# Turning q and k in separate tiles, with casts and PSUM copies split by head halves over VectorE and ScalarE

## The chip, the cores and the metric

One core of a Trainium2 chip. The metric is the device time of one execution in microseconds (us). In profile lines PE is TensorE, PEld its weight loads, DVE is VectorE, ACT is ScalarE, POOL is GpSimd. "PEclk" is the share of TensorE's full clock that was granted. SBUF and PSUM are the two on-chip memories that the program uses: PE's results are written to PSUM and copied from there to SBUF. A *tile* is a buffer that the program takes from a *pool*; the waits between instructions that use one tile are put in when the program is built (in the kernel before, ACT's copy out of a PSUM tile waits four times for DVE's copy out of it, 15.4 us in the first 85 us). A *hole* is a stretch in which PE is idle. *Bank* is the word for a size: a one-bank (single-bank) PSUM tile has 2 KB per partition (`[P, 4, 2, P]` in bf16), a two-bank tile 4 KB (`[P, 2, 4, 2, P]`).

## The reference

Sliding-window causal attention (batch 8, 8 heads, 576 tokens, head size 64, window 64), whose output of 4608 tokens x 512 goes through an up-projection to 2048, a quick GELU and a down-projection. The kernel takes and gives float32.

```python
scores = (1 / np.sqrt(D)) * np.matmul(q, k.transpose(0, 1, 3, 2))
mask = (rel >= 0) & (rel < 64)                 # rel = query position - key position
attn = softmax(np.where(mask, scores, -1e9))
x = np.matmul(attn, v).transpose(0, 2, 1, 3).reshape(B * S, H * D)
h = x @ w_in
out = (h * (1 / (1 + np.exp(-1.702 * h)))) @ w_out
```

## The kernel before

Attention works on blocks of 128 tokens (numbered m), the projections on chunks of four blocks. The program's scores take q and k with the head dimension on the partitions. For the first two batches this is done on chip. A *pair* is a load of q and k of 256 tokens (64 for a batch's third pair). It is cast to bf16 in SBUF, turned by 8 transposes of q and 8 of k on PE into PSUM, and copied from PSUM to `qkt` in SBUF. Later batches are turned by DMA and are not touched by the change.

```python
qkt = [keep.tile([P, 8, PAD + S], bf16, name=f"qkt{i}") for i in range(2)]   # q and k interleaved
DA = (nc.vector, nc.scalar)

def turn_mm(b, i, w, tiles):            # w = 0: q, 1: k
    n = pairs(i)
    for r in range(2):
        for hp in range(4):             # hp: a pair of heads
            nc.tensor.transpose(
                out=tiles[w][:, hp, r, 0:n],
                in_=rows[b % 2][w][0:n, 2 * i + r, P * hp : P * hp + P],
                identity=ident[0:n, 0:n])

def turn_out(b, i, w, tiles):           # DVE copies all of q, ACT all of k
    n = pairs(i)
    copy_on(DA[w],
        out=qkt[b % 2][:, w::2, PAD + 256 * i : PAD + 256 * i + 2 * n].rearrange(
            "p g (n r) -> p g n r", r=2),
        in_=tiles[w][:, :, :, 0:n].rearrange("p g r n -> p g n r"))

def turn_tiles(pool, tag):
    if pool is psT:                     # one tile for both: q in one half, k in the other
        t = pool.tile([P, 2, 4, 2, P], bf16, name="turn", tag=tag)
        return [t[:, 0], t[:, 1]]
    return [pool.tile([P, 4, 2, P], bf16, name="turn", tag=tag) for _ in range(2)]
# ... (scores, exp, mask, pv, norm, the turn of x, up and down) ...
```

Each engine's instructions stand in the order in which the program writes them: with the cast of the second pair written ahead of the first mask, DVE starts them at 11.01 and 11.92 us in the kernel before. Two stretches matter: the *opening* (the first four blocks, up to about 26 us), and the *seam* between the first chunk's down-projection and the second chunk's up-projection (about 47 to 63 us). `warm(n)` issues n small matmuls of no use to the result, to keep PE busy.

```python
# the seam; i counts the 16 steps of the first chunk's down-projection
        if i == 11: cast_pairs(1, 0, DA); ...
        if i == 12: turn_pairs(1, 0, turn_tiles(psT, "T"))
        if i == 14: scores(4); exp(4); down_out(0, 0); down_out(0, 1, on_dve=True); cast_v(1, 1)
        down(0, tsub, j, ...)
    mask(4); scores(5); pv(4); norm(4); exp(5)
    cast_pairs(1, 1, (nc.gpsimd, nc.scalar))
    down_out(0, 2); down_out(0, 3, on_dve=True)
    mask(5)
    x_mm(4, psT, "T"); x_out(4)
    turn_pairs(1, 1, turn_tiles(psT, "T"))
```

The softmax here doesn't subtract the row's maximum and nothing guards it: scores larger than these inputs give would overflow.

## Time and profile before

| | before |
|---|---|
| time, median of the first 3 runs (range) | 319.25 us (319.15 to 319.6) |
| profiled run: time, span, mean granted clock | 318.37 us, 316.6 us, 0.992 |
| PE's idle time in the span | 21.6 us |

The page's totals, the waits, the chain and part of the timeline are in the prediction below. What it doesn't show is the table of windows: for the opening, for the first chunk's up- and down-projection, and for the seam with what follows it, how long each engine was busy (in brackets the number of instructions).

```profile
core 0: us, PE busy (x) PEld busy (x) DVE busy (x) ACT busy (x) POOL busy (x), PEclk, DMA share, GB/s
0.00:26.00 26.00, 18.20 (x316) 15.89 (x317) 15.18 (x32) 13.30 (x16) 13.76 (x29) 0.93 1.06 207
26.00:44.00 18.00, 17.40 (x92) 9.07 (x93) 9.06 (x14) 7.76 (x13) 3.41 (x5) 1.00 1.00 218
44.00:90.00 46.00, 41.06 (x683) 32.59 (x687) 28.71 (x46) 27.86 (x43) 32.89 (x46) 1.00 0.97 177
```

No engine but PE is near full in any of these windows (PE has 17.40 of 18.00 us in the second; the fullest of the others is POOL in the third, 32.89 of 46.00), so what can be won is waiting: 7.8 us of PE's idle time lie before 26 us, 4.9 us between 44 and 90 us. Two rows of the timeline serve as landmarks (start, duration, instruction): the exponential of the first block, and the first up-projection matmuls after the scores of block 6, which end the seam.

```profile
10.10 1.02 ACT L272 ACTIVATE E<-S 128x1024 bf16<-128x1024 f32 x1 [0.50 <-PE S L262]
...
61.76 1.98 PE L349 MATMUL hps<-xT_pe,w_in_sb 128*128 128x128 bf16 x32
```

### The profile page before, as it was taken

How to read it: one execution, taken by the hardware profiler on the slowest of the kernel's cores; microseconds unless marked ns; L12 is line 12 of the kernel's file. 1: busy time of each engine (PE TensorE's matmuls, PEld its weight loads, DVE VectorE, ACT ScalarE, POOL GpSimd, SP SyncE). 2: the span in 40 equal slices, each digit the busy share in tenths (PEclk: the TensorE clock that was granted, in tenths of full speed). 3: DMA queues.
4: the chain of work that ended last, by engine and by line, in shares of the span. 5: the costliest groups of instructions: out<-in, count | busy, mean ns of one | idle time of the engine just before them, and what ended most of it. 6: DMA issues, size and time to landing. Idle time of an engine off the chain costs nothing.

```text
span 316.6 us, 7896 instructions
## 1 busy us (share of the span) xinstructions
PE 295.0 (93%) x3269; PEld 196.1 (62%) x3306; DVE 164.0 (52%) x276; ACT 157.4 (50%) x241; POOL 136.7 (43%) x195
## 2 busy tenths in 40 slices
PE   5688998599999999999999999999999999999994
PEld 5575444598777777777777777765554455444441
DVE  6556713687655555565565665555555554434300
ACT  2556514677655556545555555554444444344311
POOL 1870248474995796885669897120000000000000
PEclk9989999999999999999999999999999999999998
DMA  8999898898999999999999999955332111000121
GB/s 192 218 211 214 184 278 155 217 180 169 143 124 142 166 157 131 160 170 163 171 165 172 163 163 160 159 127 124 86 84 68 50 52 50 33 35 33 58 78 66
DMA packets 150996, 43.32 MB, mean 137 GB/s; under 512 B 135088, under 2 KB 145328, under 8 KB 150960
## 3 DMA queue, kind: packets, MB, share of 16 engines
q0 software_dynamic: 72480, 13.05, 64.1%
q1 hardware_dynamic: 74448, 22.43, 42.1%
q10 hardware_dynamic: 4032, 7.34, 6.6%
q8 instruction: 26, 0.43, 0.6%
q14 instruction: 10, 0.08, 0.1%
HBM read 36.70 MB, written 9.44 MB: 146 GB/s over the span
## 4 chain that ended last, share of the span: by engine, by line
PE 86%; ACT 4%; DVE 3%; issue 2%; DMA 2%; SPq 1%; ACTq 0%
PE ops L379 38%; PE hps L349 38%; PE Tacc L291 4%; PE S L262 4%; DMA stage_qk<-in_q_dram 2%; DVE gT L366 1%; PE turn L146 1%; ACT th L360 1%; ACT xT_pe L330 1%; DVE qkt L104 1%; PE pxt L325 1%; SPq L85 1%; ACT qkt L104 1%; DVE PT L277 1%; DVE xs L304 0%
## 5 line engine op out<-in xcount | busy, mean ns | idle before, releaser
L366 DVE SCALAR_TENSOR_TENSOR gT<-th,hps 128x512 bf16<-128x512 bf16 x144 | 98.9, 688 | 109.8 <-ACT th L360 109.6
L379 PE MATMUL ops<-w_out_sb,gT 128*128 128x512 bf16 x539 | 136.4, 379 | 5.4 <-issue 4.3
L360 ACT ACTIVATE th<-hps 128x512 bf16<-128x512 f32 x144 | 86.0, 597 | 110.7 <-PE hps L349 104.1
L349 PEld LDWEIGHTS <-w_in_sb 128*128 128x128 bf16 x1328 | 106.1, 113 | 40.9 <-issue 1.4
L379 PEld LDWEIGHTS <-gT 128*128 128x128 bf16 x576 | 53.0, 98 | 52.1 <-issue 0.8
L349 PE MATMUL hps<-xT_dma,w_in_sb 128*128 128x256 bf16 (+1 forms) x448 | 82.5, 318 | 0.0
L349 PE MATMUL hps<-xT_pe,w_in_sb 128*128 128x128 bf16 (+1 forms) x880 | 64.7, 228 | 1.1 <-ACT xT_pe L330 0.9
L272 ACT ACTIVATE E<-S 128x1024 bf16<-128x1024 f32 x36 | 36.7, 1019 | 2.7 <-PE S L262 2.7
L393 ACT ACTIVATE o_sb<-ops 128x512 f32<-128x512 f32 x34 | 20.4, 600 | 18.3 <-PE ops L379 18.0
L186 POOL COPY v_off<-v_nat 64x528 bf16<-64x528 bf16 x25 | 16.1, 646 | 27.9 <-DMA v_nat<-in_v_dram 27.3
L304 DVE TENSOR_TENSOR xs<-Tacc,rc 128x512 bf16<-128x512 f32 x36 | 24.9, 691 | 1.2
L182 POOL DMA_DIRECT2D v_nat<-in_v_dram x25 | 21.5, 859 | 2.3 <-issue 1.4
L277 DVE TENSOR_TENSOR PT<-E,mask_None 128x1024 bf16<-128x1024 bf16 x28 | 20.7, 738 | 2.4 <-ACT E L272 2.4
L181 POOL DMA_DIRECT2D rows_k<-in_k_dram x25 | 21.3, 853 | 0.0
L181 POOL DMA_DIRECT2D rows_q<-in_q_dram x25 | 21.3, 850 | 0.0
L262 PE MATMUL S<-qkt 64*128 64x64 bf16 x576 | 15.2, 191 | 3.7 <-ACT qkt L104 2.6
L291 PE MATMUL Tacc<-v_off,PT 128*64 128x65 bf16 x320 | 16.2, 198 | 1.7 <-DVE PT L277 1.7
L262 PEld LDWEIGHTS <-qkt 64*128 64x128 bf16 x576 | 10.7, 95 | 11.1 <-issue 6.0
L92 POOL CAST v_off<-stage_v 64x512 bf16<-64x512 f32 x15 | 9.9, 663 | 11.6 <-DMA stage_v<-in_v_dram 11.1
L291 PEld LDWEIGHTS <-PT 128*64 128x64 bf16 x576 | 12.2, 111 | 4.3 <-DVE PT L277 2.2
L291 PE MATMUL Tacc<-v_nat,PT 128*64 128x65 bf16 x256 | 14.4, 199 | 0.0
L188 POOL COPY v_off<-v_nat 64x528 bf16<-64x528 bf16 x20 | 12.9, 644 | 1.2
(43 smaller groups left out, 120.5 us busy)
## 6 DMA issues: line engine op xcount, KB each, us to landing
out_dram<-o_sb ACTq DMA_DIRECT2D x28, 256.0 KB, 3.2
stage_v<-in_v_dram SPq DMA_DIRECT2D x12, 256.0 KB, 6.1
rows_q<-in_q_dram POOLq DMA_DIRECT2D x20, 128.0 KB, 6.2
rows_k<-in_k_dram POOLq DMA_DIRECT2D x20, 128.0 KB, 6.9
v_nat<-in_v_dram POOLq DMA_DIRECT2D x20, 128.0 KB, 7.9
stage_qk<-in_q_dram SPq DMA_DIRECT2D x4, 512.0 KB, 5.4
stage_qk<-in_k_dram SPq DMA_DIRECT2D x4, 512.0 KB, 6.1
w_out_sb<-in_moe_w_out_dram POOLq DMA_DIRECT2D x4, 512.0 KB, 12.7
```

Source lines behind the costliest of these rows:

```text
L181: nc.gpsimd.dma_start(out=heads(rows[b % 2][w][0:n, i, :]), in_=rows_of(src, b, i))
L182: nc.gpsimd.dma_start(out=v_nat[b % 2][0:n, i, :, 0:D], in_=rows_of(v, b, i))
L262: nc.tensor.matmul(st[:, h % 2, t * 256 + hp * 64 : t * 256 + hp * 64 + 64], lhsT=src[part, 2 * hp + 1, 64 * j : 64 * j + 128], rhs=src[pa ...
L272: nc.scalar.activation(out=E_of[m][:], in_=S_of.pop(m)[:], func=AF.Exp, scale=scale)
L277: nc.vector.tensor_tensor(out=pt[:].rearrange("p a f -> p (a f)"), in0=E_of.pop(m)[:].rearrange("p a f -> p (a f)"), in1=masks[z][:].rearr ...
L291: nc.tensor.matmul(acc[t * 64 : t * 64 + 64, h // 4, (h % 4) * 66 : (h % 4) * 66 + 65], lhsT=pt[:, epos : epos + 64], rhs=win, start=True, ...
L304: nc.vector.tensor_tensor(out=xs[:].rearrange("p (b h d) -> p b h d", b=2, h=4), in0=view[:, :, :, 0:D], in1=rc[:].to_broadcast([P, 2, 4, D]),
L349: nc.tensor.matmul(ps[:, g, :], lhsT=w_in[:, c, f0 + (f + g) % 4 : f0 + 512 : 4], rhs=xT[ch][:, m0 : m0 + nt // P, c, :], start=(c == 0), ...
L360: nc.scalar.activation(out=th[:], in_=ps[:], func=AF.Tanh, scale=0.851)
L366: nc.vector.scalar_tensor_tensor(out=gT[ch, f // 4][:, f % 4 : f % 4 + nf, t0 : t0 + nt], in0=th[:], scalar=1.0, in1=ps[:], op0=ALU.add, o ...
L379: nc.tensor.matmul(O_of[ch, tsub][:, :], lhsT=gT[ch, j][:, f, tsub * P : (tsub + 1) * P], rhs=w_out_sb[:, 4 * j + f, :], start=(j == 0 and ...
L393: nc.scalar.activation(out=o_sb[:], in_=ps[:], func=AF.Copy, scale=0.5)
```

## The change

The intent: q and k get SBUF tiles of their own, and the PSUM copies, with most of the casts of the first and second pairs (not those of q in batch 0), are split by head halves, so that DVE and ACT work on one tile at the same time. Beside that, the opening and the seam are reordered (masks ahead of casts; the first pair of batch 1 turned one step earlier), the second pair of batch 1 turns in another PSUM pool, and the first weight comes in four pieces and not three.

```diff
-    qkt = [keep.tile([P, 8, PAD + S], bf16, name=f"qkt{i}") for i in range(2)]
+    qkt = [[keep.tile([P, 4, PAD + S], bf16, name=f"{w}t{i}") for w in "qk"] for i in range(2)]
 # ... cast_pair likewise takes one or two engines, one for each half of the heads ...
     def turn_mm(b, i, w, tiles):
-        for r in range(2):
-            for hp in range(4):
+        for hp in range(4):
+            for r in range(2):
     def turn_out(b, i, w, tiles):
-        copy_on(
-            DA[w],
-            out=qkt[b % 2][:, w::2, ...],
-            in_=tiles[w][:, :, :, 0:n]...,
-        )
+        for half in range(2):
+            hs = slice(2 * half, 2 * half + 2)
+            copy_on(
+                DA[half],
+                out=qkt[b % 2][w][:, hs, ...],
+                in_=tiles[w][:, hs, :, 0:n]...,
+            )
 # ... the opening ...
     scores(1)
+    mask(0)
     exp(1)
-    cast_pair(0, 1, 1, nc.scalar)
-    mask(0)
+    warm(4)
     pv(0)
+    cast_pair(0, 1, 0, nc.vector)
 # ... turn_out after x_out(0), k cast on DVE and ACT, copy of the turned x of block 2 ahead of the first tanh ...
 # ... the seam: pair (1, 0) cast at i == 10 and turned at i == 11, scores(4) at 13, mask(4) at 15 ...
-    cast_pairs(1, 1, (nc.gpsimd, nc.scalar))
-    down_out(0, 2)
+    cast_pair(1, 1, 0, nc.gpsimd, nc.vector)
+    cast_pair(1, 1, 1, nc.gpsimd, nc.scalar)
     down_out(0, 3, on_dve=True)
-    mask(5)
     x_mm(4, psT, "T")
     x_out(4)
-    turn_pairs(1, 1, turn_tiles(psT, "T"))
+    mask(5)
+    turn_pairs(1, 1, turn_tiles(psO, "O"))
```

More of the change, by code (lines that the diff above doesn't have):

```diff
@@ L61 @@
     rows = [[keep.tile([P, 6, DM], bf16, name=f"rows_{w}{i}") for w in "qk"] for i in range(2)]
-    qkt = [keep.tile([P, 8, PAD + S], bf16, name=f"qkt{i}") for i in range(2)]
+    qkt = [[keep.tile([P, 4, PAD + S], bf16, name=f"{w}t{i}") for w in "qk"] for i in range(2)]
     v_nat = [keep.tile([P, 5, H, D + 2], bf16, name=f"v_nat{i}") for i in range(2)]
     v_off = [keep.tile([P, 5, H, D + 2], bf16, name=f"v_off{i}") for i in range(2)]
-    w_in_sb = [keep.tile([P, 4, n], bf16, name=f"w_in_sb{i}") for i, n in enumerate((512, 512, 1024))]
+    w_in_sb = [keep.tile([P, 4, 512], bf16, name=f"w_in_sb{i}") for i in range(4)]
     w_out_sb = keep.tile([P, 16, DM], bf16, name="w_out_sb")
@@ L124, in load_pairs, with pair_rows, cast_pair @@
             )
-    def cast_pair(b, i, w, engine):
+    def pair_rows(b, i, w):
+        flat = rows[b % 2][w][:, 2 * i : 2 * i + 2, :].rearrange("p x e -> p (x e)")
+        return flat.rearrange("p (a r e) -> p a r e", a=2, r=2)
+    def cast_pair(b, i, w, *engines):
         n = pairs(i)
-        copy_on(
-            engine,
-            out=rows[b % 2][w][0:n, 2 * i : 2 * i + 2, :].rearrange(
-                "p r (h d) -> p h r d", d=D
-            ),
-            in_=stage_qk[(3 * b + i) % 2][0:n, w, :].rearrange(
-                "p (h r d) -> p h r d", r=2, d=D
-            ),
-        )
-    def cast_pairs(b, i, engines):
-        for w in range(2):
-            cast_pair(b, i, w, engines[w])
+        for half, engine in enumerate(engines):
+            hs = slice(half, half + 1) if len(engines) == 2 else slice(0, 2)
+            copy_on(
+                engine,
+                out=pair_rows(b, i, w)[0:n, hs].rearrange(
+                    "p a r (h d) -> p a h r d", d=D
+                ),
+                in_=stage_qk[(3 * b + i) % 2][0:n, w, :].rearrange(
+                    "p (a h r d) -> p a h r d", h=4, r=2, d=D
+                )[:, hs],
+            )
     def turn_mm(b, i, w, tiles):
         n = pairs(i)
-        for r in range(2):
-            for hp in range(4):
+        for hp in range(4):
+            for r in range(2):
                 nc.tensor.transpose(
                     out=tiles[w][:, hp, r, 0:n],
-                    in_=rows[b % 2][w][0:n, 2 * i + r, P * hp : P * hp + P],
+                    in_=pair_rows(b, i, w)[0:n, hp // 2, r, P * (hp % 2) : P * (hp % 2) + P],
                     identity=ident[0:n, 0:n],
@@ L153, in turn_out @@
         n = pairs(i)
-        copy_on(
-            DA[w],
-            out=qkt[b % 2][:, w::2, PAD + 256 * i : PAD + 256 * i + 2 * n].rearrange(
-                "p g (n r) -> p g n r", r=2
-            ),
-            in_=tiles[w][:, :, :, 0:n].rearrange("p g r n -> p g n r"),
-        )
+        for half in range(2):
+            hs = slice(2 * half, 2 * half + 2)
+            copy_on(
+                DA[half],
+                out=qkt[b % 2][w][:, hs, PAD + 256 * i : PAD + 256 * i + 2 * n].rearrange(
+                    "p g (n r) -> p g n r", r=2
+                ),
+                in_=tiles[w][:, hs, :, 0:n].rearrange("p g r n -> p g n r"),
+            )
     def turn_pairs(b, i, tiles):
@@ L193, in turn_dma @@
             nc.sync.dma_start_transpose(
-                out=qkt[b % 2][:, w::2, PAD + P * i : PAD + P * i + n],
+                out=qkt[b % 2][w][:, :, PAD + P * i : PAD + P * i + n],
                 in_=rows[b % 2][w][0:n, i, :],
@@ L198, in load_w_in @@
     def load_w_in(i):
-        f0 = 512 * i
-        f1 = DFF if i == 2 else f0 + 512
+        f = slice(512 * i, 512 * i + 512)
         nc.gpsimd.dma_start(
-            out=w_in_sb[i][:], in_=moe_w_in.rearrange("(c p) f -> p c f", p=P)[:, :, f0:f1]
+            out=w_in_sb[i][:], in_=moe_w_in.rearrange("(c p) f -> p c f", p=P)[:, :, f]
         )
@@ L233 @@
     for i in range(2):
-        nc.vector.memset(qkt[i][:, :, 0:PAD], 0.0)
+        nc.vector.memset(qkt[i][1][:, :, 0:PAD], 0.0)
         nc.vector.memset(v_off[i][0:64, 0, :, 0:D], 0.0)
@@ L263, in scores @@
                     st[:, h % 2, t * 256 + hp * 64 : t * 256 + hp * 64 + 64],
-                    lhsT=src[part, 2 * hp + 1, 64 * j : 64 * j + 128],
-                    rhs=src[part, 2 * hp, PAD + 64 * j : PAD + 64 * j + 64],
+                    lhsT=src[1][part, hp, 64 * j : 64 * j + 128],
+                    rhs=src[0][part, hp, PAD + 64 * j : PAD + 64 * j + 64],
                     start=True,
@@ L343, in up_mm @@
         ps = pool.tile([P, nf, nt], fp32, name="hps", tag=tag)
-        w_in, f0 = w_in_sb[min(f // 4, 2)], 512 if f >= 12 else 0
+        w_in = w_in_sb[f // 4]
         m0 = t0 // P
@@ L350, in up_mm @@
                     ps[:, g, :],
-                    lhsT=w_in[:, c, f0 + (f + g) % 4 : f0 + 512 : 4],
+                    lhsT=w_in[:, c, (f + g) % 4 : 512 : 4],
                     rhs=xT[ch][:, m0 : m0 + nt // P, c, :],
@@ L406 @@
     load_w_in(0)
+    cast_v(0, 2)
     load_w_in(1)
-    cast_v(0, 2)
+    cast_v(0, 3)
     load_w_in(2)
-    cast_v(0, 3)
+    load_w_in(3)
     for j in range(4):
         load_w_out(j)
-    cast_pairs(0, 0, DA)
+    cast_pair(0, 0, 0, nc.vector)
     warm(34)
@@ L419 @@
     warm(10)
+    cast_pair(0, 0, 1, *DA)
     turn_mm(0, 0, 1, tiles)
@@ L424 @@
     exp(0)
-    cast_pair(0, 1, 0, nc.vector)
     warm(10)
     scores(1)
+    mask(0)
     exp(1)
-    cast_pair(0, 1, 1, nc.scalar)
-    mask(0)
+    warm(4)
     pv(0)
+    cast_pair(0, 1, 0, nc.vector)
     norm(0)
@@ L435 @@
     mask(1)
-    turn_out(0, 1, 0, tiles)
-    warm(6)
     x_mm(0, psO, "O")
     x_out(0)
+    turn_out(0, 1, 0, tiles)
+    cast_pair(0, 1, 1, *DA)
     pv(1)
-    norm(1)
+    warm(6)
     turn_mm(0, 1, 1, tiles)
     turn_out(0, 1, 1, tiles)
+    norm(1)
     warm(8)
-    x_mm(1, psO, "O")
     scores(2)
     exp(2)
+    x_mm(1, psO, "O")
     x_out(1)
-    warm(8)
+    warm(6)
     scores(3)
+    mask(2)
     exp(3)
@@ L457 @@
     load_v(1, 1)
-    warm(6)
-    mask(2)
+    warm(4)
     pv(2)
@@ L462 @@
     u = up_mm(0, 0, 4, 0, P, wide=True)
-    u = up_th(*u)
     mask(3)
@@ L466 @@
     x_out(2)
+    u = up_th(*u)
     pv(3)
@@ L481 @@
         if i == 6:
-            cast_pairs(0, 2, GG)
+            cast_pair(0, 2, 0, nc.gpsimd)
+            cast_pair(0, 2, 1, nc.gpsimd)
             cast_v(0, 4)
@@ L488 @@
             turn_pairs(0, 2, turn_tiles(psT, "T"))
-        if i == 11:
-            cast_pairs(1, 0, DA)
+        if i == 10:
+            cast_pair(1, 0, 0, *DA)
+            cast_pair(1, 0, 1, *DA)
             cast_v(1, 0)
+            cast_v(1, 1)
             load_pairs(1, 2)
             load_v(1, 4)
-        if i == 12:
+        if i == 11:
             turn_pairs(1, 0, turn_tiles(psT, "T"))
-        if i == 14:
+        if i == 13:
+            down_out(0, 0)
             scores(4)
             exp(4)
-            down_out(0, 0)
+        if i == 15:
             down_out(0, 1, on_dve=True)
-            cast_v(1, 1)
+            mask(4)
         down(0, tsub, j, *((psO, "O") if tsub < 2 else (psH, "H")))
-    mask(4)
     scores(5)
     pv(4)
+    down_out(0, 2)
+    exp(5)
     norm(4)
-    exp(5)
-    cast_pairs(1, 1, (nc.gpsimd, nc.scalar))
-    down_out(0, 2)
+    cast_pair(1, 1, 0, nc.gpsimd, nc.vector)
+    cast_pair(1, 1, 1, nc.gpsimd, nc.scalar)
     down_out(0, 3, on_dve=True)
-    mask(5)
     x_mm(4, psT, "T")
     x_out(4)
-    turn_pairs(1, 1, turn_tiles(psT, "T"))
+    mask(5)
+    turn_pairs(1, 1, turn_tiles(psO, "O"))
     for m in range(4, 8):
@@ L533 @@
             cast_v(1, 3)
-            cast_pairs(1, 2, GG)
+            cast_pair(1, 2, 0, nc.gpsimd)
+            cast_pair(1, 2, 1, nc.gpsimd)
             cast_v(1, 4)
```

## The prediction

> **What bounds the kernel now.** I read four views in this order: the page's totals and slices, the waits of the first 85 us, the chain that ended last for the first 90 us, and the timeline of DVE, ACT and PE for the same stretch.
>
> The totals and slices say which engine and which stretch matter:
>
> ```profile
> PE 295.0 (93%) x3269; PEld 196.1 (62%) x3306; DVE 164.0 (52%) x276; ACT 157.4 (50%) x241; POOL 136.7 (43%) x195
> ...
> PE   5688998599999999999999999999999999999994
> ...
> PEclk9989999999999999999999999999999999999998
> ```
>
> A slice is 316.6 / 40 = 7.9 us. PE is at 90% or more from slice 9 (71 us) to the end but for the drain. Only slices 0 to 7 have holes: the opening (0 to 26 us, first four blocks of 128 tokens, before the first full up-projection) and the seam between the first down-projection and the second chunk (slices 6 and 7, 47 to 63 us). PE is idle 21.6 us in all, so 2% (6.4 us) would be nearly a third of all its idle time, and PE's own work does not shrink: the change has the same number of matmuls. After the last turn on PE, at about 72 us, the instructions of the two built programs stand in the same order on each engine. So only the stretch before is worked out.
>
> The waits of the first 85 us:
>
> ```profile
> ACT qkt L104 <- DVE qkt L104: 15.4, 4, 8.0
> ...
> PEld L262 <- ACT qkt L104: 3.4, 5, 1.4
> ...
> PE S L262 <- ACT qkt L104: 2.6, 4, 1.2
> ...
> PE turn L146 <- ACT xT_pe L330: 1.2, 1, 1.2
> ```
>
> The first line is the target: four times ACT's copy of the turned k (PSUM to SBUF) began only when DVE's copy of the turned q was over. Most of the 15.4 us is ACT waiting for work; what reaches PE is the third line, 2.6 us of scores waiting for ACT's copy, and the last, 1.2 us in which a turn waited for a PSUM buffer that ACT still had to empty.
>
> The timeline shows one such hand-over, at the seam, with the sizes that I use:
>
> ```profile
> 58.84 1.22 DVE L104 COPY qkt<-turn 128x1024 bf16<-128x1024 bf16 x1 [1.25 <-PE turn L146]
> ...
> 60.10 1.01 ACT L104 COPY qkt<-turn 128x1024 bf16<-128x1024 bf16 x1 [2.40 <-DVE qkt L104]
> ...
> 61.16 0.29 PE L262 MATMUL S<-qkt 64*128 64x64 bf16 x8 [1.25 <-ACT qkt L104]
> ```
>
> And the opening's other bound, in the chain of the first 90 us: a transfer issued at 4.81 us, after which DVE does a cast and only then the first mask, though that mask's input was ready at 11.12 us.
>
> ```profile
> 4.81 6.17 DMA stage_qk<-in_q_dram
> ...
> 11.01 0.99 DVE rows_q L104
> 12.00 1.02 DVE PT L277
> ```
>
> [...] each ACT half waits for DVE's half of the same tile, not for PE. Only a run can show what that costs. [...] DVE's turned copy is 1223 ns for 1024 elements and 422 ns for 256, so 1.043 ns an element and 155 ns fixed; ACT's is 1012 and 372 ns, so 0.833 ns and 159 ns fixed. [...] in the trace the cast on DVE is 0.69 us alone and 0.99 us beside POOL's casts, the mask 0.68 and 1.09 us. I keep the slow size for the first mask.
>
> **Sizes (estimates from those rows).** DVE copy of 512 elements 0.69 us, of 128 elements 0.29; ACT 0.585 and 0.265. ACT's cast of 1024 takes 1.04, so of 512 about 0.61; DVE's 0.69 becomes about 0.42. A hand-over costs 0.02 to 0.05 us.
>
> **The change, part by part.**
>
> *Copies split by head halves.* The intent is that DVE and ACT empty a tile together. [...] a tile is emptied in 0.69 + 0.585 + 0.02 = 1.30 us, against 1.22 on DVE alone or 1.01 on ACT alone. What is left is a pipeline: with q and k in tiles of their own, DVE can empty half of k while ACT has half of q. Where both lie in one two-bank tile (the turns made in the pool of two-bank accumulators: the third pair of batch 0 and the first and third of batch 1), the built order has DVE's k half waiting for ACT's q half: four copies in a row.
>
> *First pair (opening).* q turned by 6.37 as now; DVE's half to 7.06, ACT's to 7.66. ACT can cast its half of k only then, to 8.27, where today it casts all of k from 6.83 to 7.87. [...] DVE waits for the last transpose, 8.74; it copies to 9.43, ACT to 10.04. Today ACT's copy ends at 9.60. The remaining scores put the first exponential at 10.45 instead of 10.10: +0.35. Part of it is hidden by the next point.
>
> *Mask before cast.* The mask now goes ahead of the cast of the second pair: 11.49 to 12.5, so the first PV is at 12.55 instead of 13.06 (-0.5). DVE then casts q to 13.2, normalises to 14.13 (today 14.51), masks to 14.76 (15.11).
>
> *Second pair.* DVE's half of q 14.7 to 15.4, its half of k's cast to 15.85; ACT's half of q to 16.0 and of k's cast to 16.6, where today ACT had cast all of k by 13.91. k is turned at 17.1, DVE to 17.8, ACT to 18.4; today 17.83. The scores of block 2 finish late, its exponential starts at 18.8 instead of 18.45 (+0.35). From here the order is nearly the old one; doing the copy of block 2 ahead of the tanh gives back a little. I get the last up-projection of block 3 at 26.2 instead of 25.93: **+0.26 us for the opening**.
>
> *Seam, first pair of batch 1.* Four copies in a row take 0.69 x 2 + 0.585 x 2 + 0.06 = 2.61 us against 1.23 + 1.01 + 0.02 = 2.26. They start one group of four matmuls earlier (0.87 us), but so do the scores that need them (group 13, not 14). I get the scores' second half free at 51.74 with 12 matmuls to go, today 52.26 with 8 to go: block 5's scores at 54.65 instead of 54.31, +0.34.
>
> *Seam, second pair.* Its tiles now lie in the single-bank pool, so PE need not wait for ACT to empty the x tile (the 1.2 us wait above), and the casts are halved between POOL, DVE and ACT. Worked through: normalised block 4 at 56.42; its transposes 56.47; up-projection 57.6 instead of 58.64. DVE first does an output copy to 57.56 and mask 5 to 58.3, then q to 59.0 and k to 59.7; ACT 59.02 to 59.6, 59.72 to 60.31. The scores' second half is free at 60.35 (today 61.16) and PE goes on at 60.6 instead of 61.38: **-0.78 us for the seam**, the +0.34 being included.
>
> *Third pair of batch 1 (around 71 us).* Four small copies, 0.29 x 2 + 0.265 x 2 + 0.06 = 1.17 us against 0.42 + 0.37 + 0.03 = 0.82: **+0.36 us**, on a path where PE waits 0.32 already.
>
> *Weights in four pieces.* The second piece is issued at about 16.9 instead of 13.9 us, being behind POOL's cast of a v tile. The issues before took 5.4 to 10.1 us to land; it is needed at about 27. Nothing.
>
> Sum: 0.26 - 0.78 + 0.36 = -0.16 us.
>
> **Rivals.** *The halves do overlap.* Then a turned pair takes about 0.7 us a tile, three 128-wide turns gain 0.5 to 1 us each and the order another 1: 316 to 317 us. For it: the intent, and 2.6 us of scores waiting. Against it: the waits in the built program. *The clock.* The granted clock was 0.83 in 12 to 16 us and 0.75 in 16 to 20 us, after PE's 1.48 us hole at 11.6. [...] In that stretch eight transposes took 1.04 instead of 0.61 us; with the hole at 13 us shrunk, the chain from PV 1 to scores 2 could lose 0.5 us: 318.5. Against it: the new waits for ACT's halves open holes of their own, which could as well cost 0.5. *ACT becomes the bound.* Every pair now gives ACT four instructions in order, each behind DVE; if one lands behind an exponential (1.02 us), scores wait that much longer: 320 to 320.5. *A late weight:* if the delayed issue made PE wait at 27 us, 1 to 2 us more; nothing in the trace has PE waiting for weights.
>
> **Range and chances.** 319.25 - 0.16 is 319.1; I shade it to 318.9 because the order was presumably tried and the clock rival points down. The three terms are each good to about 0.6 us, the clock and the contention to 0.7, together some 1.3; times 1.28 that is 1.7, and I lengthen the lower side for the overlapping rival: 316.8 to 320.6. Beyond 2% would take 6.4 us, from a stretch of 90 us in which PE is idle 13.3 us (busy 76.7) and does filler matmuls for another 6 or so: 3% for faster, 2% for slower, 95% within.
>
> **What would show it.** Right: in the waits, ACT's copies still wait for DVE's; four rows of 512-element copies in a row at about 49 to 52 us, of 0.69 and 0.585 us; the first exponential at about 10.45; scores of block 6 going on near 60.5; the wait of a turn for the x copy gone; PE busy time unchanged at 295 us. Wrong: DVE and ACT reading the halves at the same time; the first exponential at or before 10.1; a granted clock near 1 from 12 to 20 us; PE waiting for a weight transfer near 27 us; or any change of rate after 90 us, which nothing here accounts for.

That two engines don't empty one tile together was read off the built order alone ("each ACT half waits for DVE's half of the same tile"). That DVE's half of k waits for the last transpose was the author's estimate; the changed kernel's waits have it (`DVE kt L104 <- PE turn L149: 2.6, 2, 1.3`). The slow size of the first mask rests on rows of the trace alone (0.68 us, and 1.09 with POOL's cast beside it). That the clock follows PE's holes was not shown; the 0.5 us of that rival is the author's estimate, beside the 1.04 - 0.61 = 0.43 us of the eight transposes.

## The result and the profile after

| | before | after |
|---|---|---|
| time, median of 4 (range) | 319.2 us (319.05 to 319.6) | 318.54 us (318.42 to 319.04) |
| ratio | | 0.998 [0.9963, 0.9998] |
| profiled run: time, span, mean clock | 318.37 us, 316.6 us, 0.992 | 318.44 us, 316.6 us, 1.000 |

A ratio here and below is the mean time of one kernel's fast runs over that of the other's of the same rounds, with a 95% interval in square brackets, so it is not quite the ratio of the medians that are quoted. The change is within 2%. The two profiled runs have the same span. All outputs are right.

The totals and slices of the page after:

```profile
PE 296.1 (94%) x3269; PEld 195.8 (62%) x3306; DVE 164.8 (52%) x286; ACT 157.0 (50%) x248; POOL 137.6 (43%) x197
...
PE   6778999799999999999999999999999999999994
...
PEclk9999999999999999999999999999999999999999
```

PE runs the same number of matmuls (its busy time reads 1.1 us more). The opening is a little fuller, the hole of slices 6 and 7 has shrunk (from 8 and 5 tenths busy to 9 and 7), and no slice shows a lowered clock. The windows after:

```profile
0.00:26.00 26.00, 18.64 (x314) 15.39 (x315) 14.93 (x36) 12.28 (x18) 14.82 (x30) 1.00 1.04 194
26.00:44.00 18.00, 17.05 (x90) 8.95 (x91) 9.48 (x14) 8.06 (x14) 3.41 (x5) 1.00 0.94 205
44.00:90.00 46.00, 42.17 (x685) 32.91 (x689) 30.02 (x52) 28.28 (x48) 32.26 (x47) 1.00 1.05 190
```

The waits of the first 85 us after (total us, times, longest):

```profile
ACT qt L104 <- DVE qt L104: 18.3, 6, 7.8
...
ACT kt L104 <- DVE kt L104: 3.9, 5, 1.2
...
PE S L266 <- DVE kt L104: 2.0, 5, 0.7
...
PE S L266 <- ACT kt L104: 1.5, 4, 0.4
...
DVE kt L104 <- ACT qt L104: 1.3, 3, 0.7
```

The wait of ACT for DVE, which the change was to remove, is still there, and there are more of them: eleven (6 and 5) where there were four. PE's scores wait 2.0 + 1.5 = 3.5 us for the copies where they waited 2.6. The last line shows the chain turned round as well: DVE waits for ACT.

The timeline after: the first transposes, the first exponential, the first pair of batch 1, and the end of the seam:

```profile
5.85 1.04 PE L149 MATMUL turn<-ident,rows_q 128*128 128x128 bf16 x8 [0.61 <-DVE rows_q L104]
...
11.00 1.02 ACT L276 ACTIVATE E<-S 128x1024 bf16<-128x1024 f32 x1 [0.45 <-PE S L266]
...
49.50 0.69 DVE L104 COPY qt<-turn 128x512 bf16<-128x512 bf16 x1 [1.59 <-PE turn L149]
...
50.22 0.59 ACT L104 COPY qt<-turn 128x512 bf16<-128x512 bf16 x1 [2.06 <-DVE qt L104]
...
50.84 0.69 DVE L104 COPY kt<-turn 128x512 bf16<-128x512 bf16 x1 [0.65 <-ACT qt L104]
...
51.56 0.59 ACT L104 COPY kt<-turn 128x512 bf16<-128x512 bf16 x1 [0.76 <-DVE kt L104]
...
61.36 1.98 PE L353 MATMUL hps<-xT_pe,w_in_sb 128*128 128x128 bf16 x32
```

Each of the four copies starts 0.03 us after the one before it is over: four in a row, never two at once. The first exponential is 0.90 us late, the end of the seam 0.40 us early. After the third turn (72.45 us before, 72.40 us after) the two kernels run alike to the end.

One thing lies between the medians and the profiles: the clock. In the 33 runs of the kernel before that went with the experiments, the six with a mean clock under 0.988 took 319.98 us on average, the 15 from 0.988 to below 0.992 took 319.26, and the 12 at 0.992 or more took 318.62. Nine of ten runs of the changed kernel had 0.997 or more, and those nine average 318.65 us (the tenth, at 0.992, took 321.59). So the changed kernel at a full clock takes what the kernel before takes when its clock is good; its small lead in the median goes with the clock that it keeps more steadily. At an equal clock it may even be the slower one: only two of the 33 runs before had 0.997 or more, and they took 317.82 and 317.86 us, less than any run of the changed kernel (318.29 at the least). This is a reading of the runs' records and was not tested by itself.

### The profile page after: what moved, and what is told of

Its sections match the earlier page's. It is cut to its first block, busy times and chain, and to the rows that moved or that the text cites. A ratio compares the mean times of both kernels' runs of the same rounds, so it can differ in the third digit from the quotient of the medians.

```text
span 316.6 us, 7923 instructions
## 1 busy us (share of the span) xinstructions
PE 296.1 (94%) x3269; PEld 195.8 (62%) x3306; DVE 164.8 (52%) x286; ACT 157.0 (50%) x248; POOL 137.6 (43%) x197
## 4 chain that ended last, share of the span: by engine, by line
PE 84%; DVE 6%; ACT 5%; issue 2%; DMA 2%; ACTq 0%
PE hps L353 37%; PE ops L383 37%; PE Tacc L295 4%; PE S L266 4%; DMA stage_qk<-in_q_dram 1%; DVE gT L370 1%; DVE PT L281 1%; PE turn L149 1%; ACT th L364 1%; DVE qt L104 1%; ACT kt L104 1%; ACT qt L104 1%; DMA out_dram<-o_sb 1%; DVE kt L104 1%; ACT xT_pe L334 1%
## 5 line engine op out<-in xcount | busy, mean ns | idle before, releaser
L191 POOL COPY v_off<-v_nat 64x528 bf16<-64x528 bf16 x25 | 16.4, 658 | 15.9 <-DMA v_nat<-in_v_dram 15.4
L266 PE MATMUL S<-qt,kt 64*128 64x64 bf16 x576 | 16.1, 191 | 4.5 <-DVE kt L104 2.0
L266 PEld LDWEIGHTS <-kt 64*128 64x128 bf16 x576 | 11.0, 95 | 12.5 <-issue 6.2
```

The costliest lines, as they stand in the source:

```text
L266: nc.tensor.matmul(st[:, h % 2, t * 256 + hp * 64 : t * 256 + hp * 64 + 64], lhsT=src[1][part, hp, 64 * j : 64 * j + 128], rhs=src[0][part ...
```

## The experiments

Each kernel ran 5 rounds against the kernel before, in three sets of different chips. "Before" is its median in the same set: 319.07 us in the first set, 319.05 in the second, 318.89 in the third.

My theory was: DVE and ACT empty one PSUM tile in turn, since the program's ordering lets only one of them at it, so the split gains nothing and costs, with every extra instruction, the part that doesn't shrink with its size (by the prediction's fit to copies of two sizes, 155 ns on DVE and 159 on ACT); what the order gains pays for that. The rival was that the parts are each worth nothing, and a second was that it is the shared *SBUF* tile that makes ACT wait in the kernel before.

### First set: the parts apart, and the halves in tiles of their own

**split_only**: the split casts and copies, the separate tiles and the four weight pieces, in the order of the kernel before.

```diff
 # against the changed kernel: the order goes back, for instance
-    mask(0)
     exp(1)
-    warm(4)
+    mask(0)
     pv(0)
-        if i == 11:
+        if i == 12:
             turn_pairs(1, 0, turn_tiles(psT, "T"))
-    turn_pairs(1, 1, turn_tiles(psO, "O"))
+    turn_pairs(1, 1, turn_tiles(psT, "T"))
```

> The kernel before with the split casts and copies and separate q and k tiles, but its old order. Theory (the halves wait for each other, so the split by itself costs time and the order pays): slower than before by 1 to 2 us in all (about +0.7 at the exponential of block 2, +0.35 at each of the three turns that share a two-bank tile), ratio to before 1.003 to 1.006, some 320.2 to 321 us. Rival (the split is what gains, the order adds little): at or below the changed kernel, ratio 0.998 or less.

Measured: 321.61 us (320.32 to 323.59), ratio 1.0071 [1.0038, 1.0105]. The split (with the tiles and weight pieces) in the old order makes the kernel slower, by some 2.5 us, a little more than expected. Part of this goes with the clock: in its profile, the slowest of its six runs, the granted clock was 0.79 from 54 to 64 us, and 16 matmuls of the up-projection took 1.91 us there, against 1.06 in the changed kernel.

**order_only**: the changed kernel's order, pools and separate tiles, but whole copies and casts.

```diff
     def turn_out(b, i, w, tiles):
-        for half in range(2):
-            hs = slice(2 * half, 2 * half + 2)
-            copy_on(DA[half], out=qkt[b % 2][w][:, hs, ...], in_=tiles[w][:, hs, :, 0:n]...)
+        copy_on(DA[w], out=qkt[b % 2][w][:, :, ...], in_=tiles[w][:, :, :, 0:n]...)
 # ... and each cast whole on one engine, k of (0,0) and (0,1) on ACT as before ...
```

> The changed kernel's order, tiles and pools, but q copied and cast whole on DVE and k whole on ACT as before. Theory: the order gains more without the split; the exponential of block 2 at about 17.3 us instead of 18.9 in the changed kernel, scores of block 6 complete about 59.5 instead of 60.8 because whole copies from two one-bank tiles run side by side; 2 to 3 us below before, ratio 0.990 to 0.994. Rival (the split gains): slower than the changed kernel, ratio 0.999 to 1.002.

Measured: 315.74 us (315.0 to 316.32), ratio 0.9887 [0.9863, 0.9911]. Everything but the split (the order, the new pool of one pair, the SBUF tiles, the weight pieces) is worth about 3.3 us together. These were not taken apart here, and "the order" below means all of them. The rival that the parts are worth nothing is out: they are a gain and a loss that nearly cancel.

**halves_own_bank**: the changed kernel with the PSUM tiles grouped by half and not by q and k, so that DVE's halves of q and k lie in one tile and ACT's in another. The number and size of all instructions stay the same.

```diff
-                    out=tiles[w][:, hp, r, 0:n],
+                    out=tiles[hp // 2][:, w, hp % 2, r, 0:n],
 ...
-                in_=tiles[w][:, hs, :, 0:n].rearrange("p g r n -> p g n r"),
+                in_=tiles[half][:, w, :, :, 0:n].rearrange("p g r n -> p g n r"),
 ...
-            t = pool.tile([P, 2, 4, 2, P], bf16, name="turn", tag=tag)
-            return [t[:, 0], t[:, 1]]
-        return [pool.tile([P, 4, 2, P], bf16, name="turn", tag=tag) for _ in range(2)]
+            return [pl.tile([P, 2, 2, 2, P], bf16, name="turn", tag=tg)
+                    for pl, tg in ((psT, "T"), (psS, "S"))]
+        return [pool.tile([P, 2, 2, 2, P], bf16, name="turn", tag=tag) for _ in range(2)]
```

> The changed kernel with each half (of q and of k together) turned into a tile and bank of its own, so that DVE and ACT can empty halves at the same time; nothing else changed. Theory [...]: no wait of ACT's copy for DVE's is left, the first exponential comes about 0.6 us earlier than in the changed kernel, the first pair of batch 1 is emptied in about 1.4 us instead of 2.6; 2 to 3.5 us below before, ratio 0.989 to 0.994. Rival (the fixed cost of more, smaller instructions eats the gain, or the gain is hidden behind other waits): within 0.5 us of the changed kernel, ratio 0.997 to 0.999.

(What this run tests is the common tile.)

Measured: 313.85 us (313.54 to 314.16), ratio 0.9826 [0.9802, 0.9849]: the fastest of this set, and faster than expected (0.989 to 0.994). The wait that the change was meant to remove is now gone; in its place ACT waits for PE, that is, for work. The view of waits of this kernel, and then its timeline at the first pair of batch 1:

```profile
ACT qt L104 <- PE turn L149: 14.5, 4, 7.5
```

```profile
47.67 0.69 DVE L104 COPY qt<-turn 128x512 bf16<-128x512 bf16 x1 [2.19 <-PE turn L149]
...
47.90 0.58 ACT L104 COPY qt<-turn 128x512 bf16<-128x512 bf16 x1 [2.12 <-PE turn L149]
...
48.28 0.68 DVE L104 COPY kt<-turn 128x512 bf16<-128x512 bf16 x1
...
48.38 0.59 ACT L104 COPY kt<-turn 128x512 bf16<-128x512 bf16 x1
```

The same four copies of the same sizes now lie beside each other: they end 48.97 - 47.67 = 1.30 us after the first begins, against 52.15 - 49.50 = 2.65 us in the changed kernel. Its opening ends early too: the first exponential starts at 9.27 us, with no change in the order. In the changed kernel's profile it starts at 11.00 us, but there the first eight transposes took 1.04 us, here 0.78; turn11_in_T below, with the changed kernel's opening and transposes of 0.62 us, has it at 10.50 us, so at least 1.2 us come from the tiles. So it is the common PSUM tile that made the split a loss. (This run doesn't show what in a common tile asks for the order.)

**turn11_in_T**: the changed kernel with the second pair of batch 1 turned in the old pool, to size that part alone.

```diff
-    turn_pairs(1, 1, turn_tiles(psO, "O"))
+    turn_pairs(1, 1, turn_tiles(psT, "T"))
```

> The changed kernel with the second pair of batch 1 turned in the two-bank accumulator tile again, as before. Theory (half of the seam's gain comes from this pool): PE waits again for ACT's copy of x, four copies in a row, scores of block 6 complete at about 61.7 instead of 60.8; 0.7 to 1.2 us above the changed kernel, ratio to before 1.000 to 1.002. Rival (the seam's gain comes from the halved casts and the order): no change, ratio 0.998.

Measured: 320.97 us (320.32 to 321.85), ratio 1.0048 [1.0023, 1.0073], against about 318.6 us for the changed kernel in the other sets. One line takes back 2.4 us, twice the wait of 1.2 us that the line removed, and more than expected (0.7 to 1.2 us). The windows from 54 us on of this kernel, then its timeline, show the rest:

```profile
54.00:64.00 10.00, 7.70 (x116) 5.95 (x115) 7.04 (x12) 5.35 (x8) 7.10 (x10) 0.74 0.76 190
64.00:70.00 6.00, 5.96 (x109) 5.67 (x108) 3.76 (x8) 3.78 (x6) 4.51 (x8) 0.86 1.07 174
```

```profile
58.11 0.61 PE L149 MATMUL turn<-ident,rows_q 128*128 128x128 bf16 x8 [0.67 <-ACT xT_pe L334]
...
59.12 1.91 PE L353 MATMUL hps<-xT_pe,w_in_sb 128*128 128x128 bf16 x16
...
63.02 3.21 PE L353 MATMUL hps<-xT_pe,w_in_sb 128*128 128x128 bf16 x32
```

PE waits 0.67 us for ACT to empty the x tile, and then runs at a lowered clock (0.74, then 0.86): 16 matmuls take 1.91 us, and 32 take 3.21 us where the changed kernel needs 1.98. The waiting opened a hole, and the clock fell behind it; whether the holes are the cause is the subject of the third set. That was not in my sum.

### Second set: where the wait of the kernel before comes from, and two versions built on the findings

**before_apart**: the kernel before, whole copies, with the PSUM tile of 4 KB per partition made two tiles of 2 KB. q and k still share their SBUF tile.

```diff
         if pool is psT:
-            t = pool.tile([P, 2, 4, 2, P], bf16, name="turn", tag=tag)
-            return [t[:, 0], t[:, 1]]
+            return [pl.tile([P, 4, 2, P], bf16, name="turn", tag=tg)
+                    for pl, tg in ((psT, "T"), (psS, "S"))]
```

> The kernel before with one edit: where q and k are turned into one two-bank accumulator tile, they go into two one-bank tiles (the second from the scores' pool); q and k still share one SBUF tile, nothing is split or reordered. Theory (the waits of ACT's copy for DVE's came from the shared PSUM tile, not from the shared SBUF tile): none of those waits is left, scores of block 4 complete about 0.5 us earlier, of block 6 about 1.2 us more, of block 8 about 0.3; 1.5 to 2.2 us below before, ratio 0.993 to 0.996. Rival (the SBUF tile that q and k share is what orders them, as the change's words have it): no change, ratio 0.999 to 1.001.

Measured: 317.12 us (315.86 to 317.6), ratio 0.9935 [0.9899, 0.997]. Its waits:

```profile
ACT qkt L104 <- PE turn L146: 13.5, 5, 7.5
```

ACT waits for DVE's copy in no case any more, although the SBUF tile is still shared. For the first pair of batch 1, DVE copies from 48.97 to 50.20 us and ACT from 49.41 to 50.42; in the kernel before, ACT's copy began at 51.19, 0.03 us after the end of DVE's. So the waits of 15.4 us in the kernel before came from the common PSUM tile, not from the common SBUF tile. In that tile q and k had separate halves (`t[:, 0]` and `t[:, 1]`), and the two copies read nothing in common: in these runs the program orders its accesses to PSUM by the tile.

**whole_apart**: order_only with the same edit.

> The order-only kernel with the same edit: q and k of the turns in the accumulator tile go into two one-bank tiles. Theory: two more waits go (about 0.6 us at the first pair of batch 1, 0.35 at its third pair), 0.7 to 1 us below the order-only kernel, ratio to before 0.985 to 0.987. Rival (those waits are hidden by the down-projection's matmuls): ratio as the order-only kernel, 0.988 to 0.989.

Measured: 314.45 us (314.02 to 316.02), ratio 0.9858 [0.9825, 0.9892]. With order_only still having this wait (first fence: its line in the waits; second: that of whole_apart), separate PSUM tiles give order_only a further gain of about 1 us by the medians, though the two intervals overlap.

```profile
ACT kt L104 <- DVE qt L104: 12.1, 3, 8.0
```

```profile
ACT kt L104 <- PE turn L149: 12.5, 5, 7.5
```

Whole copies in separate tiles (0.9858 [0.9825, 0.9892]) and halves in separate tiles (0.9826 [0.9802, 0.9849]) can't be told apart by these intervals: most of what halves_own_bank wins is had without cutting anything in halves.

**turn11_in_T_filler**: turn11_in_T with filler matmuls in the two holes ahead of the turn (12 before the turn of x, 8 after its copy). Theory: with the holes filled the clock holds, and about half of the loss comes back.

```diff
     down_out(0, 3, on_dve=True)
+    warm(12)
     x_mm(4, psT, "T")
     x_out(4)
+    warm(8)
     mask(5)
```

> The kernel that turns the second pair of batch 1 in the accumulator tile, with 20 filler matmuls in the PE's holes of the seam; it waits for the same things. Theory (of its 2.4 us over the changed kernel some 1 is the wait and the rest the granted clock, which fell to 0.87 in 44 to 64 us): the clock stays at or near 1 there, the up-projection after scores 6 takes about 2.0 us instead of 3.2, about 1 us above the changed kernel, ratio 1.000 to 1.002. Rival (it is all waiting): no change, ratio 1.004 to 1.006.

Measured: 322.17 us (321.28 to 323.5), ratio 1.0098 [1.0063, 1.0133]. A miss. In the profile PE kept its full speed up to 60 us (16 matmuls of the up-projection in 1.06 us again), and the clock fell one hole later (0.92 granted in 54 to 64 us, 0.85 in 64 to 70 us): between 60.1 and 62.0 us PE had only eight short scores matmuls, and the 32 matmuls behind them took

```profile
62.28 3.52 PE L353 MATMUL hps<-xT_pe,w_in_sb 128*128 128x128 bf16 x32
```

So the theory was neither shown nor refuted: the fillers were not where the last hole was. Why this kernel timed slower than the one without fillers is open.

**holes_filled**: halves_own_bank with two holes closed by order alone: the turn of block 3's x moved one up-projection group ahead, and the second pair of batch 1 cast on POOL alone and turned before block 4's x.

```diff
-    up(0, 0, 4, 2 * P, P, wide=True)
     x_mm(3, psT, "T")
     x_out(3)
+    up(0, 0, 4, 2 * P, P, wide=True)
 # ...
-    cast_pair(1, 1, 0, nc.gpsimd, nc.vector)
-    cast_pair(1, 1, 1, nc.gpsimd, nc.scalar)
-    down_out(0, 3, on_dve=True)
+    cast_pair(1, 1, 0, nc.gpsimd)
+    cast_pair(1, 1, 1, nc.gpsimd)
+    tiles = turn_tiles(psO, "O")
+    # turn_mm of q and k
     x_mm(4, psT, "T")
     x_out(4)
+    # turn_out of q and k
+    down_out(0, 3, on_dve=True)
     mask(5)
-    turn_pairs(1, 1, turn_tiles(psO, "O"))
```

> The halves-in-own-banks kernel with two holes of PE filled: the x transposes of block 3 go between two up-projections instead of after them, and the second pair of batch 1 is cast on POOL alone and turned while block 4 is normalised. Theory (PE's holes at about 24 and 54 us are on the path, 0.94 and 1.06 us): 0.8 to 1.8 us below that kernel, some 312 to 313 us, ratio 0.977 to 0.980. Rival (the next wait takes their place): ratio 0.982 to 0.983.

Measured: 312.6 us (312.16 to 315.81), ratio 0.9814 [0.9769, 0.9859]; four of its five runs lie between 312.16 and 313.11 us. It has the best median of all, but the gain is smaller than expected, the verdict on its ratio is unclear, and its interval overlaps that of halves_own_bank, so this last step is not settled by the timing. In its profile the seam ends at 56.21 us, against 57.73 in halves_own_bank. A new wait appears there, of 0.4 us for a weight piece, just ahead of the first up-projection matmuls, which neither the kernel before nor the changed one had: these matmuls start at 19.07 us here, against 20.68 and 21.11, early enough for a transfer to reach the path.

### Third set: what the clock takes

**t11_again** is turn11_in_T once more, **seam_filled** adds to it the fillers of turn11_in_T_filler and 24 more in the hole where the clock had fallen, and **changed_again** is the changed kernel, all on one chip.

```diff
 # seam_filled, against turn11_in_T_filler
         u = up_mm(1, 0, 4, t0, P, wide=True)
+        if m == 4:
+            warm(24)
         scores(m + 2)
```

> The kernel that turns the second pair of batch 1 in the accumulator tile, unchanged, so that the next run has it on the same chip: ratio to before 1.003 to 1.007 as before, granted clock below 1 somewhere in 54 to 70 us.

> The same kernel with 44 filler matmuls in the PE's holes of the seam, 24 of them in the hole that the first filler run left (while PE waits for the four copies before scores 6). Theory (the granted clock falls because of those holes, and with it goes more time than the wait): the clock stays at 1.00 in 54 to 70 us, the up-projection after scores 6 takes about 2.0 us instead of 3.2 to 3.5, and the run is 1 to 1.7 us below the kernel without fillers. Rival (the clock is given by something else, or fillers cost what they save): no difference of over 0.4 us.

> The changed kernel itself on the chip of these runs, five rounds: ratio to before 0.997 to 0.999, 0.4 to 1.0 us below it. If the change is worth nothing, 0.999 to 1.001; and 2 to 3 us below the kernel with the turn in the accumulator tile.

| | median (range), us | ratio to before | granted clock, 54 to 64 us |
|---|---|---|---|
| t11_again | 321.67 (319.92 to 322.51) | 1.0077 [1.0047, 1.0107] | 0.83 |
| seam_filled | 320.14 (319.48 to 321.0) | 1.0042 [1.0017, 1.0067] | 1.00 |
| changed_again | 318.75 (318.29 to 321.59) | 1.0007 [0.9974, 1.0039] | 1.00 |

The clocks are those of the profiled runs. The timeline of t11_again, and then that of seam_filled:

```profile
60.09 1.91 PE L353 MATMUL hps<-xT_pe,w_in_sb 128*128 128x128 bf16 x16
...
63.58 1.98 PE L353 MATMUL hps<-xT_pe,w_in_sb 128*128 128x128 bf16 x32
...
109.23 0.29 PE L266 MATMUL S<-qt,kt 64*128 64x64 bf16 x8 [1.10 <-DMA kt<-rows_k]
```

```profile
59.45 1.06 PE L353 MATMUL hps<-xT_pe,w_in_sb 128*128 128x128 bf16 x16
...
60.34 1.50 PE L404 MATMUL idle<-ident 128*128 128x128 bf16 x24
...
62.95 1.98 PE L353 MATMUL hps<-xT_pe,w_in_sb 128*128 128x128 bf16 x32
```

With the holes filled, the clock stays at 1.00 and the 16 matmuls keep their full speed; the 32 behind them were at full speed in t11_again already, where the clock had fallen earlier than in turn11_in_T. The medians differ by 321.67 - 320.14 = 1.5 us, the means by 1.15, and the two intervals just overlap (1.0047 against 1.0067). The two profiles show less: the seam ends 63.58 - 62.95 = 0.63 us earlier, and 1.10 us of the rest is a wait of t11_again for a DMA at 109 us (its last row above), which seam_filled doesn't have and which the fillers were not meant to touch. So in these four profiles the clock held where the holes were filled: it fell in the three without this filling (0.74 in turn11_in_T, 0.92 in turn11_in_T_filler, 0.83 in t11_again, from 54 to 64 us) and not in this one (1.00). The length of a hole alone doesn't decide: in turn11_in_T holes of 1.06 and 0.67 us came before the fall, while the kernel before had holes of 1.06 and 1.19 us at the same place, at a clock of 1.00. What the fall costs is about 0.7 us by this pair of profiles, and 1.75 us where it lasts longer (39.81 - 38.06, turn11_in_T against seam_filled, in the stretch below).

The stretch from the last up-projection of block 3 to the second group of up-projection matmuls behind the seam gives the same sizes without the opening: 37.05 and 37.00 us in the two profiles of the changed kernel, 38.06 in seam_filled, 38.79 in t11_again and 39.81 in turn11_in_T. Going back to the old pool thus costs about 1.0 us at a full clock (the wait, and whatever the fillers add), and 0.7 to 1.8 us more where the clock falls.

changed_again puts the changed kernel at 1.0007 of the kernel before, where the first comparison had it at 0.998: whether it gains anything at all stays open. (One of its six runs, at 321.59 us, lifts the mean; its median is 0.14 us below that of the kernel before.)

## Why the prediction was right, and which of its steps were not

The predicted 318.9 us and the class held: 318.54 us, and 318.75 us on another chip. The landmarks of the profiles (start in us) show where the terms stand. The last two columns are worked out from the others.

| landmark | before | after | order_only | halves_own_bank | order's share (order_only - before) | the halves' share (after - order_only) |
|---|---|---|---|---|---|---|
| last up-projection of block 3 | 25.93 | 26.35 | 25.22 | 24.75 | -0.71 | +1.13 |
| end of the seam | 61.76 | 61.36 | 58.45 | 57.73 | -3.31 | +2.91 |
| up-projection after the third turn | 72.45 | 72.40 | 69.13 | 68.20 | -3.32 | +3.27 |

1. *Opening, +0.26.* Measured 26.35 - 25.93 = +0.42. The sign is right; that the size is so near is luck. The terms inside were further off: the first exponential came 0.90 us later (+0.35 predicted), the first PV 0.23 us earlier (0.5), the exponential of block 2 0.48 us later (0.35). And one profile doesn't fix this landmark so closely: it lies at 26.18 to 26.93 us in six profiles with the changed opening, at 25.41 and 25.93 in two with the old one.
2. *Seam, -0.78.* Measured (61.36 - 61.76) - 0.42 = -0.82. Its steps fit too. Less the 0.42 us of the opening, block 5's scores are at 54.64 us (54.65 predicted), block 4's transposes at 56.49 (56.47), the up-projection at 57.83 (57.6), and the last copy is over at 60.35 (60.31).
3. *Third turn, +0.36.* From the end of the seam to the landmark after it: 11.04 us after, 10.69 before, +0.35.
4. *The sum, -0.16 us.* The profiles give -0.05 us at the last landmark, and equal spans.
5. *The mechanism: DVE and ACT do not empty one tile together.* The waits and the four copies in a row show it, with the sizes of the prediction (0.69 and 0.59 us). The experiments confirm it as the cause: when the halves got tiles of their own, the ratio went from about 1 to 0.9826. What the runs show is that the built program orders accesses by the tile.

What failed, by its own steps:

- *"Where both lie in one two-bank tile ... the built order has DVE's k half waiting for ACT's q half"* was read off rightly, but without asking why. before_apart shows that whole copies of q and k, which lay in separate halves of the tile, were ordered one after the other just because they had one tile: with two, none of ACT's four waits for DVE's copy (15.4 us) is left. Because I took the tile's layout for given, I never asked what the layout was worth: 2 us of the kernel before's time, by one edit that cuts nothing in halves. That the SBUF tiles were separated was not the point either.
- *The rival "the halves do overlap", 316 to 317 us.* It was rightly held to be unlikely for this program, but mis-sized: made to happen, it is 313.85 us. The prediction gave each of the three 128-wide turns 0.5 to 1 us and the order 1 us; order_only has the order, with the pool and the rest of the change, worth 3.3 us, most of it in the seam (-2.60 of -3.31). Part of that is again separate PSUM tiles: the new pool gives q and k of the second pair two.
- *The pool of the second pair, "the 1.2 us wait above".* The path through the seam that rests on it came out right, but the wait is not all that the pool is worth. Taking the pool change back costs 2.4 us in one set and 2.9 us in another: in the profiles about 1.0 us at a full clock, and 0.7 to 1.8 us that came with a lowered one. The prediction counted a hole of PE as long as it was, and not with what may happen to the matmuls after it.
- *First exponential at 10.45 us.* It came at 11.00 us, and at 10.85 in the second profile of the changed kernel. The first eight transposes ran slowly in these runs (1.04 us, where the prediction had 0.62 from the kernel before): the 34 fillers ahead of them took 3.81 us, 112 ns each, against 62 ns for each of the 24 in seam_filled, so PE was slow at the start, though PEclk reads 1.00 there. When it comes up to speed differs between profiles: the first eight transposes took 0.62 us in the kernel before and in turn11_in_T, 0.78 in halves_own_bank and 1.03 in t11_again. In split_only and turn11_in_T, whose casts and turn of that pair are the same, the first exponential came at 10.56 and 10.50 us. *The first mask* took 0.72 us and not 1.0; POOL's last cast beside it ended 0.17 us after it began.
- *The clock rival, 318.5 us.* The clock in 12 to 20 us did rise, from 0.83 and 0.75 to 1.00, which the prediction had named as a sign of being wrong. The opening ended later all the same: order_only, with the same order and 1.00 there too, ends it 1.13 us earlier, of which the slow first transposes explain 0.42 and the split the rest. Nor is the rise sure: of six profiles with these very instructions up to 26 us, three have 1.00 in that stretch (after, changed_again, turn11_in_T_filler: the landmark at 26.18 to 26.35 us), and three 0.79 to 0.87 (turn11_in_T, t11_again, seam_filled: 26.48 to 26.93 us).
- *ACT as the bound* and *a late weight* did not happen: the last landmark is not later than before, and PE waits for no weight in the changed kernel.

So a result near zero was the sum of a gain of some 3.3 us and a loss of about the same size. The prediction followed the one path that the built program takes and got its net right; what the two parts are worth by themselves it did not see.

## What to carry to other kernels

Before an operation is split over two engines, look at which PSUM tile both would read: if it is one tile, as here, the program's waits put them in a row, and two instructions cost more than one (q's two halves in the changed kernel's opening: 6.93 to 8.24, 1.31 us; the whole copy on DVE before: 1.23). Group the tile by the engine that empties it, and the same instructions run side by side (four copies in 1.30 us, against 2.65). When a change moves nothing, run its parts alone, for a gain and a loss may hide in it. And price a hole on PE with the clock that it may cost the matmuls behind it (0.7 to 1.8 us at this seam), not just with its length.
